# Loading decay weights as columns, doing the first decays in halves and moving an A product ahead of a broadcast, at the start of a fused RWKV-5 and MLP kernel

## The chip, the cores and the metric

One core of a Trainium2 chip (trn2). The metric is the device time of one execution in microseconds (us). Most executions agree within 0.3%, and the differences here are about 1% or less, so every experiment was timed beside the kernel before, in five rounds for most and three for e12.

Engines in the profile's lines: PE is TensorE, PEld its weight loads, DVE is VectorE, ACT is ScalarE, POOL is GpSimd, SP the sync engine, and a "q" behind a name is an engine's sequencer or queue. L12 is line 12 of that kernel's own file, so line numbers differ by a few between kernels.

## The reference, cut to what matters

```python
# r, k, v: (4 batches, 8 heads, 768 steps, 48); w, u: (8, 48)
for t in range(S):
    cur = np.einsum('bhd,bhe->bhde', u[None] * kt, vt)
    y[:, :, t] = np.einsum('bhd,bhde->bhe', rt, state + cur)
    state = w[None, :, :, None] * state + np.einsum('bhd,bhe->bhde', kt, vt)
# x: y as (3072, 384)
h = x @ w_in                       # w_in (384, 2048)
out = (h * (1.0 / (1.0 + np.exp(-h)))) @ w_out
```

The kernel works in chunks of 128 steps, 24 units (6 chunks by 4 batches). For each unit it decays r and k by powers of w, forms A = k r per head, masks it, and multiplies it with v; the term with u is the row sum of r (k u), times v. The MLP products fill TensorE between units.

## The kernel before

Only the start is touched. The tiles, the loads and the spins (products of zeros, there to get TensorE up to full pace):

```python
    wrow = cst.tile([NP, 2, 64], FP)
    urow = cst.tile([NP, 2, 64], FP)
    junk = cst.tile([128, 512], F16)
    nc.vector.memset(junk, 0.0)
    for t in (wrow, urow):
        nc.vector.memset(t[:, :, D:64], 1.0)
    ...
    load_row(wrow, w)
    load(0, mid=lambda: load_row(urow, u))      # r, k, u, v of unit 0 on the sync queue
    for i in range(1, B):
        load(i)
    ...
    spin(5)
    wT = to_cols(wrow, None)                    # transpose on TensorE
    spin(4)
    ...
    nc.vector.tensor_copy(out=pi[:, 0:NP, 1:2], in_=wT.unsqueeze(2))
    ...                                         # seven doublings: the powers of w and 1/w, "pif"
```

A spin is called cold here when the next one starts 0.43 us after it, and warm at 0.22 us. The granted-clock column of the profile reads 1.00 over these cold microseconds too, so in the first microseconds cold and warm are read from the spacing alone.

The two phases of a unit that matter, and the order in which unit 0 and 1 run:

```python
    def p1(i, mid=None, spins=0):               # r, k transposed, then decayed
        ...
        nc.vector.tensor_tensor(out=L["rT"], in0=tr[0:PR], in1=lamR, op=ALU.mult)
        if mid:
            mid()
        nc.vector.tensor_tensor(out=L["kT"], in0=tk[0:PR], in1=lamK, op=ALU.mult)
    # p2(i): A on TensorE into ae, ao; VectorE evicts both (copies them out) through the mask (am)
    # nat_ku, nat_rk: k*u and r*(k*u) on GpSimd; bonus_sum: row sums (rku) on VectorE
    ...
    p1(0, mid=to_cols_u)                        # u as a column, then "the rows of u": u repeated
                                                # on 128 partitions by TensorE; ScalarE copy: u_bc
    nat_v(0)
    ...                                         # lamCT on ScalarE
    nc.gpsimd.tensor_copy(out=gate, in_=rin[1][:, 0, 0:1])   # makes GpSimd wait for unit 1's r
    win_part(0, 512)                            # GpSimd issues a quarter of w_in
    nat_ku(0)
    nat_rk(0)
    p2(0)
    p1(1, spins=1)
    bonus_sum(0)
    nat_ku(1)
    nat_rk(1)
    nat_v(1)
    p3y(0)                                      # y of unit 0 on TensorE
    ...
    bonus_sum(1)
    bonus_vu(1)
    p2(1, spins=2)
    p3e(0)
    spin(4)
    p3y(1)
```

## Time and profile before

| | before |
|---|---|
| time, median of 4 runs | 201.77 us (201.52 to 202.05) |
| span of the profiled execution | 200.2 us |
| PE busy | 192.0 us, 96% |
| unit 0's r and k decays begin | 6.60 us |
| u's rows ready (u_bc) | 7.46 us |
| GpSimd's first ku begins | 8.75 us |
| unit 1's A eviction begins | 13.39 us |
| first MLP product begins | 17.13 us |

Times inside a span count from its first instruction. From 17 us on TensorE is the bound, and the rows from the decays down are the steps that lead there. Their profile lines stand in the prediction.

### The profile page before, as it was taken

The numbers are of one execution on the slowest core, as the hardware profiler recorded it, in microseconds if no ns is written. First come the engines' busy times: TensorE is split into PE (matmuls) and PEld (weight loads), VectorE is DVE, ScalarE is ACT, GpSimd is POOL, SyncE is SP. The second block draws the span as 40 slices with busy tenths as digits, with TensorE's granted clock in tenths as the row PEclk, the third lists the DMA queues.
The fourth block names the chain that finished last, engine by engine and source line by source line (L and its number), as shares of the span: only waits on it lengthen the run. The fifth ranks groups of instructions, "written<-read, shape, count | busy, mean of one in ns | idle before, by whom it ended". The sixth has DMA issues, their size and how long they took to land.

```text
span 200.2 us, 5013 instructions
## 1 busy us (share of the span) xinstructions
PE 192.0 (96%) x1973; PEld 129.8 (65%) x1973; DVE 115.1 (58%) x233; ACT 97.9 (49%) x225; POOL 115.2 (58%) x145
## 2 busy tenths in 40 slices
PE   7789999898999999999999999999999999999993
PEld 2546878786776976765666765666764666644563
DVE  6787658894757647773746864646863635510121
ACT  2655487798133652049662039662039661069300
POOL 3489969989865783768593767481748370100000
DMA  4999998999889954498521748201120001210022
GB/s 86 201 185 165 181 213 178 178 186 194 170 172 226 245 120 97 103 221 175 114 48 40 163 114 161 43 0 43 39 84 0 0 3 41 78 43 0 0 79 79
DMA packets 82207, 22.34 MB, mean 112 GB/s; under 512 B 75400, under 2 KB 82184, under 8 KB 82184
## 3 DMA queue, kind: packets, MB, share of 16 engines
q1 hardware_dynamic: 78504, 18.88, 43.7%
q0 software_dynamic: 3680, 3.15, 10.3%
q8 instruction: 15, 0.25, 0.5%
q14 instruction: 8, 0.07, 0.1%
HBM read 20.45 MB, written 4.72 MB: 126 GB/s over the span
## 4 chain that ended last, share of the span: by engine, by line
PE 84%; DVE 6%; POOL 4%; issue 3%; ACT 1%; DVEq 0%; POOLq 0%
PE ops L366 30%; PE hps L354 28%; PE ae L267 10%; PE xs L242 4%; PE y L293 3%; PE yT L342 2%; DVE am L276 2%; PE y L290 2%; POOL ku L180 1%; PE ops L380 1%; PE sps L309 1%; PE spin L125 1%; DVE pif L156 1%; POOL rku_f L186 1%; DVE y L300 1%
## 5 line engine op out<-in xcount | busy, mean ns | idle before, releaser
L357 ACT ACTIVATE gT<-hps 128x256 f16<-128x256 f32 (+1 forms) x128 | 59.5, 495 | 25.1 <-PE hps L354 23.3
L354 PE MATMUL hps<-xT,win 128*128 128x256 f16 (+1 forms) x384 | 69.9, 326 | 0.2
L366 PE MATMUL ops<-wout,gT 128*128 128x384 f16 x368 | 65.8, 326 | 0.0
L354 PEld LDWEIGHTS <-win 128*128 128x128 f16 x384 | 35.2, 98 | 22.1 <-issue 0.9
L366 PEld LDWEIGHTS <-gT 128*128 128x128 f16 x368 | 34.2, 98 | 20.9
L343 ACT COPY xT<-yT 128x384 f16<-128x384 f16 x24 | 11.5, 478 | 56.4 <-PE yT L342 56.4
L276 DVE TENSOR_TENSOR am<-ae,maskM 128x512 f16<-128x512 f32 x24 | 16.6, 691 | 32.5 <-PE ao L269 32.5
L203 POOL TENSOR_TENSOR vu<-vin,rku 128x384 f32<-128x384 f32 x23 | 19.1, 829 | 21.8 <-DVE rku L197 21.7
L370 DVE COPY osb<-ops 128x384 f32<-128x384 f32 x23 | 12.8, 556 | 32.5 <-PE ops L366 32.3
L267 PE MATMUL ae<-rk 48*128 48x128 f32 x192 | 27.7, 285 | 1.0 <-DVE rk L230 1.0
L267 PEld LDWEIGHTS ae<-rk 48*128 48x128 f32 x192 | 23.1, 187 | 8.3 <-issue 5.8
L269 PE MATMUL ao<-rk 48*128 48x128 f32 x192 | 27.7, 285 | 0.0
L253 DVE TENSOR_TENSOR rk<-xs,pif 112x512 f32<-112x512 f32 x40 | 25.6, 680 | 1.7 <-PE xs L242 1.7
L180 POOL TENSOR_TENSOR ku<-kin,u_bc 128x384 f32<-128x384 f32 x24 | 24.1, 1005 | 2.0 <-DMA kin<-in_k_dram 2.0
L186 POOL TENSOR_TENSOR rku_f<-rin,ku 128x384 f32<-128x384 f32 x24 | 24.1, 1005 | 1.9
L191 POOL TENSOR_TENSOR kc<-kin,lamC 128x384 f16<-128x384 f32 x24 | 24.0, 1002 | 0.0
L269 PEld LDWEIGHTS ao<-rk 48*128 48x128 f32 x192 | 23.1, 187 | 0.0
L323 POOL CAST stb<-st 112x384 f16<-112x384 f32 x12 | 6.0, 502 | 22.8 <-DVE st L318 22.8
L300 DVE TENSOR_TENSOR y<-y,vu 128x384 f16<-128x384 f32 x24 | 13.3, 554 | 8.7 <-PE y L293 6.5
L276 DVE TENSOR_TENSOR am<-ao,maskM 128x512 f16<-128x512 f32 x24 | 16.3, 680 | 0.0
L197 DVE TENSOR_REDUCE rku<-rku_f 128x8 f32<-128x384 f32 x24 | 13.2, 549 | 2.4 <-POOL rku_f L186 2.0
L325 POOL TENSOR_TENSOR sdec<-st,pif 112x384 f32<-112x384 f32 x16 | 13.3, 835 | 1.8 <-ACT gT L357 1.1
(74 smaller groups left out, 188.4 us busy)
## 6 DMA issues: line engine op xcount, KB each, us to landing
rin<-in_r_dram SPq DMA_DIRECT2D x24, 192.0 KB, 4.0
kin<-in_k_dram SPq DMA_DIRECT2D x24, 192.0 KB, 3.8
vin<-in_v_dram SPq DMA_DIRECT2D x24, 192.0 KB, 3.8
out_dram<-osb SPq DMA_DIRECT2D x23, 192.0 KB, 2.0
win<-in_moe_w_in_dram POOLq DMA_DIRECT2D x4, 384.0 KB, 6.0
wout<-in_moe_w_out_dram POOLq DMA_DIRECT2D x2, 768.0 KB, 10.4
out_dram<-osh SPq DMA_DIRECT2D x1, 128.0 KB, 1.7
out_dram<-osh SPq DMA_DIRECT2D x1, 64.0 KB, 1.5
```

What stands on the lines that cost most here:

```text
L180: nc.gpsimd.tensor_tensor(out=L["ku"], in0=kin[i % NIN][:, :, 0:D], in1=u_bc, op=ALU.mult)
L186: nc.gpsimd.tensor_tensor(out=L["rku_f"], in0=rin[i % NIN][:, :, 0:D], in1=L["ku"], op=ALU.mult)
L191: nc.gpsimd.tensor_tensor(out=kc[i % NKC][:, :, 0:D], in0=kin[n][:, :, 0:D], in1=lamC, op=ALU.mult)
L203: nc.gpsimd.tensor_tensor(out=L["vu"], in0=vin[i % NIN], in1=L["rku"].unsqueeze(2).broadcast_to([128, H, D]), op=ALU.mult)
L253: nc.vector.tensor_tensor(out=rk[:, :, :, 64 * g:64 * g + 64], in0=xs[g][0:PR], in1=lam(g), op=ALU.mult)
L267: nc.tensor.matmul(ae[:, p, :], L["kT"][0:D, p, :], L["rT"][0:D, p, :], start=True, stop=True)
L269: nc.tensor.matmul(ao[:, p, :], L["kT"][64:PR, p, :], L["rT"][64:PR, p, :], start=True, stop=True)
L276: nc.vector.tensor_tensor(out=am, in0=a, in1=maskM.unsqueeze(1).broadcast_to([128, NP, C]), op=ALU.mult)
L300: nc.vector.tensor_tensor(out=L["y16"], in0=L["y"], in1=L["vu"], op=ALU.add)
L354: nc.tensor.matmul(hps, win[:, q, ft * 128:(ft + 1) * 128], xts[sc][:, q, b0:b1, :].rearrange("p b t -> p (b t)"), start=(q == 0), stop=(q ...
L357: nc.scalar.activation(out=gts[sc][:, ft, b0 * C:b1 * C], in_=hps, func=AF.Silu)
L366: nc.tensor.matmul(ops, gts[sc][:, ft, b * C:(b + 1) * C], wout[:, ft, :], start=(ft == 0), stop=(ft == NFT - 1))
```

## The change

The intent: w arrives already as columns, so that no transpose and no wait for spins stands ahead of its powers; the first A product can start when half of the head pairs are decayed; and A goes ahead of the rows of u on TensorE so that it isn't held up by them.

```diff
-    wrow = cst.tile([NP, 2, 64], FP)
+    wcol = cst.tile([PR, NP], FP)
 ...
-    for t in (wrow, urow):
-        nc.vector.memset(t[:, :, D:64], 1.0)
+    nc.vector.memset(urow[:, :, D:64], 1.0)
+    nc.vector.memset(wcol[32:64, :], 1.0)
 ...
-    load_row(wrow, w)
+    for j, e in ((0, nc.sync), (1, nc.scalar)):
+        e.dma_start(out=wcol[64 * j:64 * j + D, :],
+                    in_=bass.AP(tensor=w.tensor, offset=D * j, ap=[[1, D], [PW, NP]]))
 ...
-    spin(5)
-    wT = to_cols(wrow, None)
-    spin(4)
+    spin(10)
 ...                                             # wT = wcol; in p1:
-        nc.vector.tensor_tensor(out=L["rT"], in0=tr[0:PR], in1=lamR, op=ALU.mult)
-        if mid:
-            mid()
-        nc.vector.tensor_tensor(out=L["kT"], in0=tk[0:PR], in1=lamK, op=ALU.mult)
+        step = NP // 2 if i == 0 else NP
+        for q in range(0, NP, step):
+            q = slice(q, q + step)
+            for x, t, lam_ in (("rT", tr, lamR), ("kT", tk, lamK)):
+                nc.vector.tensor_tensor(out=L[x][:, q], in0=t[0:PR, q], in1=lam_[:, q],
+                                        op=ALU.mult)
 ...
-    p1(0, mid=to_cols_u)
+    p1(0)
+    ucol = to_cols(urow, nc.scalar.copy)
+    p2(0)
+    to_rows(u_bc, lambda p: ucol[:, p:p + 1].broadcast_to([PR, 128]))
 ...
-    p2(0)
```

## The prediction

> **What bounds the kernel now.** I read the page first, then the merged chain of work that ended last, then the timeline of each engine over the first 17 us, because the diff touches nothing that runs later. The page's first part says what the rest of the run is:
>
> ```profile
> PE 192.0 (96%) x1973; PEld 129.8 (65%) x1973; DVE 115.1 (58%) x233; ACT 97.9 (49%) x225; POOL 115.2 (58%) x145
> ```
>
> TensorE is busy 96% of 200.2 us, and a table by stretches gives it 21.9 of 22.9 us between 17.1 and 40 and all of the time between 60 and 150. Its program order is fixed. So what the start loses or wins before about 17 us, where the first product of the MLP begins, should reach the end nearly one for one. The question is only when that point comes. The merged chain, start and duration in its first two columns, shows the path to it:
>
> ```profile
> 3.57 0.20 PE cols L129
> 3.79 0.17 DVE pif L152
> ...
> 6.60 0.70 DVE rk L226
> ...
> 8.76 1.01 POOL ku L180
> 9.84 1.00 POOL rku_f L186
> 10.84 0.96 POOL ku L180
> 11.89 1.01 POOL rku_f L186
> 12.92 0.55 DVE rku L197
> 13.47 1.21 DVE am L276 x2
> 14.72 0.35 PE y L293 x7
> ```
>
> The reader is to see two parts. To 7.3 us it is w: its transpose, the powers of w (pif), the decay of r and k (rk). From 8.76 to 12.9 it is GpSimd: two units' k times u and r times that. VectorE does unit 1's row sums (rku) ahead of its A eviction (am) in program order, so am waits for GpSimd, and so does y of unit 1. What GpSimd's first ku waited for is in its own timeline and in ScalarE's:
>
> ```profile
> 6.98 0.48 ACT L149 COPY u_bc<-rows 128x384 f32<-128x384 f32 x1 [0.69 <-PE rows L147]
> ```
>
> ```profile
> 7.67 0.19 POOL L430 COPY gate<-rin 128x1 f32<-128x1 f32 x1 [4.94 <-DMA rin<-in_r_dram]
> 7.79 0.93 POOL L413 DMA_DIRECT2D win<-in_moe_w_in_dram  x1
> 8.75 1.01 POOL L180 TENSOR_TENSOR ku<-kin,u_bc 128x384 f32<-128x384 f32 x1
> ```
>
> The rows of u were ready at 7.46, but GpSimd first waits for unit 1's r (7.67) and then issues a part of w_in for 0.93 us. So u had 1.3 us to spare. The chain names ScalarE's casts as the step before ku; that I read as an artefact, since the issue of a transfer is not counted as busy. VectorE's idle time confirms that unit 1 waited for GpSimd and not the reverse:
>
> ```profile
> 9.14 0.69 DVE L276 TENSOR_TENSOR am<-ae,maskM 128x512 f16<-128x512 f32 x1 [1.25 <-PE ao L269]
> ...
> 12.92 0.55 DVE L197 TENSOR_REDUCE rku<-rku_f 128x8 f32<-128x384 f32 x1 [0.83 <-POOL rku_f L186]
> ```
>
> VectorE sat idle 0.83 us for GpSimd. Unit 0's A eviction at 9.14 could come 0.8 us earlier and nothing would follow sooner.
>
> **What the Trainium skill says.** (1) DMA: Bandwidth & Descriptors, Rules for kernel authors: a strided last dimension becomes one descriptor per element. The w columns are such a load: 48 partitions by 4 single floats, 192 descriptors on each of two queues, against 8 pieces of 192 bytes before. No run of before has a load of this kind. (2) The same page, Where the ~2 µs actually goes: most of a small transfer's time is the confirmation of the last write, hardly its size. The trace agrees: w's packets moved at 2.33 to 2.45 us in the transfer view, but its transpose began at 3.50 though the weight-load engine had been idle 0.84 us; issued at 0.81, w took about 2.65 us, while unit 0's r, 128 times the bytes, took 2.7. (3) VectorE: DVE Perf Modes, the section on the TRN2 errata: each instruction pays a fixed cost beside its elements. The trace agrees: in the chain of powers 112x512 takes 0.70 us and 112x256 0.44, so 0.18 of fixed cost when dependent; independent 112x512 decays start 0.60 us apart. (4) TensorE: Matmul & The Clock Gate, Part 1: a cold array runs at half rate for about 3.4 us of work. The trace agrees at the start: the first spins' weight loads are 0.43 us apart (1.66, 2.09, 2.52), and the later ones closer.
>
> **The change part by part.**
>
> *w as columns.* Removed: the transpose on TensorE (3.50 to 3.77) and the wait of TensorE's five cold spins ahead of it. Added: a second queue and a wait. The built program's order shows what the diff does not: the column load on the sync queue waits for VectorE's memset of rows 32 to 64 of the same tile (rows 32 to 48 overlap). That is the third memset; the second started at 1.19 before, so the load is issued at about 1.30 in place of 0.81. With 2.65 us to landing it lands at 3.95. If the 0.82 us of the first issue was partly start-up (later issues took 0.42 to 0.66), take off up to 0.4; for 12 single-element descriptors per engine at the page's mean of 17.8 ns per packet (43.7% of 16 x 200.2 us over 78504 packets; an estimate) and the other queue's as many, add 0.2 to 0.4. I take 3.9, and the start of the powers at 3.95 against 3.79: **+0.15 us**. The ScalarE queue's half, issued near 0.8, should be there by 3.6. All r, k, u, v loads stand behind the waiting one and move 0.1 to 0.5 us later; r lands near 4.7 and k near 5.5, still ahead of the decay.
>
> *Decay in halves.* The powers take 2.68 us as before (3.79 to 6.47), so the decay begins at 6.6 + 0.15 = 6.75. Four instructions of half the size at about 0.35 us each: the first half of r and k is done at 7.45, the second at 8.15 (one pair of full size before: 1.2 us and ends at 7.9). The A product's first half runs 7.5 to 8.1 beside the second decays; its second half, half of the 1.15 us that eight pairs took before (7.95 to 9.10) plus a restart, runs 8.2 to 8.9. A's eviction starts near 8.95, against 9.14: **-0.2 us**, off the path.
>
> *A ahead of the rows of u.* This is the part that costs. The rows of u stood in TensorE's gap at 6.34, before the decay was done. Now they follow the second half of A: transposes from 8.75, 0.64 us until ScalarE starts (6.34 to 6.98 before), 0.48 for the copy: u is ready at about **9.9 instead of 7.46**. GpSimd is free at 8.75 plus what unit 1's r is late, say 9.0. So ku starts at 9.9 in place of 8.75, **+1.15 us**, and u has become its releaser.
>
> *Ten spins in one run.* Nine and a transpose become ten without a gap. Spins 6 to 8 stay cold, two run warm: end near 4.9, as the r transposes need r anyway: 0.
>
> *What follows.* From ku of unit 0 to the end of the second rku_f was 8.75 to 12.89 = 4.14 us, all GpSimd: now about 14.0; unit 1's sums 14.05, its A eviction 14.6 against 13.47, and y of unit 1 and all TensorE work behind it about 1.1 us later. ScalarE's casts and lamCT slide too (lamCT from 8.95 to 11.4, which holds the lamC transposes and unit 1's A product to about 13.3), still less than GpSimd's path. GpSimd itself gets back 0.58 us, its wait for unit 2's k at 15.07, but TensorE is then already late. Sum: +1.15 on the path, minus perhaps 0.1 absorbed later. 201.92 + 1.0 = **202.9 us**.
>
> **The rivals.** *It wins as intended* (the w part lands early and the A product releases everything): if both halves landed by 3.1, just after VectorE's memsets end at 2.96, the powers start 0.7 us sooner, the rows of u are ready at 9.2, and ku starts 0.4 late instead of 1.1. For a real gain the path from rku to am would have to be VectorE's own; the 0.83 us idle speaks against it. Time: 201.3 to 202.2. *It is absorbed*: GpSimd's waits for unit 2's k (0.58) and unit 4's k (1.43 us at 26.7) take up its delay and TensorE's fillers hide the rest. For it: DMA is at 98% or more through most of the first 17 us. Against it: y of unit 1 stands in front of the fillers in TensorE's fixed order, and TensorE idles under 1 us between 17 and 40. Time: about 202.0. *The columns are slow*: 4-byte descriptors from the two queues land 0.5 to 1 us later than I think and hold unit 0's r as well; every step above moves by that. Time: 203.5 to 204.
>
> **Range and chances.** The order of the built program makes u late in every case; the size hangs on the landing of w, between 3.2 and 4.6, that is -0.7 to +0.7 on 202.9. With a small chance that the delay is absorbed, the 8-in-10 range is 202.0 to 203.8. 2% is 4 us, far from any case here: within 2% 0.97, faster 0.01, slower 0.02. That it is above the time before I hold at 85%.
>
> **What would show it.** Right: the sync queue's w load starting at about 1.3; powers starting near 3.95; four decays of about 0.35; u's copy on ScalarE ending near 9.9 and GpSimd's first ku following it at once; VectorE idle before unit 1's rku well over 0.83 us; the first MLP product near 18.2 instead of 17.13. Wrong: powers starting before 3.4; ku of unit 0 at 8.8 or earlier; or all of that as predicted and the first MLP product, or the span, unmoved.

## The result, and the profile after

203.23 us (median of 4 runs, 202.92 to 203.40) against 201.77: the ratio is 1.0070, with a 95% interval of 1.0051 to 1.0090. Ratios here and below are the mean time of one kernel's runs over that of the other's of the same rounds, so not quite the ratio of the medians quoted. Executions over 1.5% slower than the fastest of the same kernel are left out of the means. Clear of noise it is 0.7% slower, 1.4 us. The granted clock of the profiled run is 0.999, so the two spans, 201.5 and 200.2 us, compare.

GpSimd's timeline of the changed kernel (start, duration, instruction, in brackets the idle time ahead of it and what ended it):

```profile
7.63 0.19 POOL L430 COPY gate<-rin 128x1 f32<-128x1 f32 x1 [4.90 <-DMA rin<-in_r_dram]
7.75 0.93 POOL L410 DMA_DIRECT2D win<-in_moe_w_in_dram  x1
10.15 1.00 POOL L179 TENSOR_TENSOR ku<-kin,u_bc 128x384 f32<-128x384 f32 x1 [1.46 <-ACT u_bc L147]
```

The gate and the issue stand where they were; ku comes at 10.15 in place of 8.75, after 1.46 us of idleness that u's copy ends. ScalarE's line for that copy, whose end is 9.58 + 0.48 = 10.06:

```profile
9.58 0.48 ACT L147 COPY u_bc<-rows 128x384 f32<-128x384 f32 x1 [2.12 <-PE rows L145]
```

VectorE's timeline of the changed kernel, in the order of the steps:

```profile
3.34 0.17 DVE L151 COPY pif<-wcol 112x4 f32<-112x4 f32 x1 [0.21 <-DMA wcol<-in_w_dram]
...
6.65 0.42 DVE L230 TENSOR_TENSOR rk<-tr,pif 112x256 f32<-112x256 f32 x1 [0.65 <-PE tr L222]
...
9.04 0.69 DVE L277 TENSOR_TENSOR am<-ae,maskM 128x512 f16<-128x512 f32 x1 [0.80 <-PE ao L270]
...
14.31 0.55 DVE L196 TENSOR_REDUCE rku<-rku_f 128x8 f32<-128x384 f32 x1 [1.49 <-POOL rku_f L185]
14.78 0.68 DVE L277 TENSOR_TENSOR am<-ae,maskM 128x512 f16<-128x512 f32 x1
```

Unit 0's A is evicted at 9.04 instead of 9.14, so the change did what it was meant to do there, by 0.1 us. Unit 1's sums wait 1.49 us for GpSimd, up from 0.83, and unit 1's A is evicted at 14.78 instead of 13.39. The two things that I had not expected are in the first two lines: the powers start at 3.34, earlier than before (3.79), but the decay then waits 0.65 us for the r transposes. TensorE's timeline says why:

```profile
1.26 4.45 PE L127 MATMUL spin<-junk 128*128 128x512 f16 x10 [1.26 <-DVE junk L80]
5.50 1.06 PE L222 MATMUL tr<-ident,rin 128*112 128x128 f32 x4
6.35 0.77 PE L222 MATMUL tk<-ident,kin 128*112 128x128 f32 x4
...
18.53 0.49 PE L355 MATMUL hps<-xT,win 128*128 128x256 f16 x3
```

All ten spins ran cold and the r transposes took 1.06 us. In the profile of the kernel before, the transposes began at 4.82 and four of them took 0.60 us:

```profile
4.82 0.60 PE L223 MATMUL tr<-ident,rin 128*112 128x128 f32 x4
...
17.13 0.49 PE L354 MATMUL hps<-xT,win 128*128 128x256 f16 x3
```

The first MLP product, 17.13 before, is at 18.53: 1.40 us later, which is the loss in the time.

### The profile page after: what moved, and what is told of

Same layout as the page of the kernel before. It is cut to its first block, busy times and chain, and to the rows that moved or that the text cites. A ratio compares the mean times of both kernels' runs of the same rounds, so it can differ in the third digit from the quotient of the medians.

```text
span 201.5 us, 5014 instructions
## 1 busy us (share of the span) xinstructions
PE 193.8 (96%) x1973; PEld 131.1 (65%) x1973; DVE 115.4 (57%) x235; ACT 97.7 (48%) x225; POOL 115.2 (57%) x145
## 3 DMA queue, kind: packets, MB, share of 16 engines
q0 software_dynamic: 3680, 3.15, 10.4%
## 4 chain that ended last, share of the span: by engine, by line
PE 83%; issue 6%; POOL 5%; DVE 4%; ACT 1%; POOLq 0%; DVEq 0%
PE ops L367 30%; PE hps L355 28%; PE ae L268 10%; PE xs L243 4%; PE y L294 3%; PE yT L343 2%; DVE am L277 2%; PE y L291 2%; POOL ku L179 1%; PE ops L381 1%; PE sps L310 1%; POOL rku_f L185 1%; DVE y L301 1%; PE ao L270 1%; DVE rku L196 1%
```

## The experiments

All are correct against the reference. "ku" is the start in the profile of unit 0's first GpSimd product with u, or of rku_f where ku was moved to VectorE.

| run | what it is | ku, us | time, us | ratio to before (95%) |
|---|---|---|---|---|
| the change | | 10.15 | 203.23 | 1.0070 (1.0051 to 1.0090) |
| e1 | change, u ahead of A | 8.60 | 201.72 | 0.9992 (0.9980 to 1.0004) |
| e2 | w part alone | 8.48 | 201.79 | 0.9996 (0.9983 to 1.0009) |
| e3 | before, GpSimd delayed 1 us | 9.79 | 202.74 | 1.0053 (1.0028 to 1.0077) |
| e4 | order part alone | 10.25 | 203.93, two groups | 1.0101 (1.0080 to 1.0122) |
| e7 | e4, eight spins later on | 10.25 | 203.34 | 1.0079 (1.0066 to 1.0092) |
| e10 | change, eight spins | 9.44 | 202.47 | 1.0030 (1.0016 to 1.0044) |
| e6 | before, ku on VectorE | (8.68) | 201.60 | 0.9987 (0.9975 to 0.9999) |
| e8 | e2, ku on VectorE | (8.83) | 201.15 | 0.9971 (0.9959 to 0.9983) |
| e5 | e1, ku on VectorE | (9.59) | 201.11 | 0.9970 (0.9950 to 0.9991) |
| e9 | e5, eight spins | (8.77) | 201.06 | 0.9958 (0.9946 to 0.9971) |
| e11 | e8, eight spins | (8.55) | 201.06 | 0.9957 (0.9945 to 0.9970) |
| e12 | before, three spins then six | 8.93 | 201.96 | 1.0007 (0.9990 to 1.0024) |

My theory after the result: the loss is u reaching GpSimd late, and nothing else. The rivals: the cold spins and late transposes (the w part) cost it, or the halves do.

**e1, the changed kernel with u's rows ahead of A again.**

```diff
-    p2(0)
     to_rows(u_bc, lambda p: ucol[:, p:p + 1].broadcast_to([PR, 128]))
+    p2(0)
```

> The changed kernel with one thing undone: the rows of u stand ahead of unit 0's A product again. Theory (the loss is u reaching GpSimd late, 10.15 in place of 8.75 us): the u column is transposed near 7.05 as in the changed kernel, its rows near 7.6, ScalarE's copy ends near 8.7, so GpSimd's first ku starts at 8.7 to 8.9 and the time is 201.6 to 202.1 us, all of the loss gone. Rival (the loss is the cold spins, the late r transposes or the halves): ku may come early, but the time stays at 202.8 us or more.

201.72 us, and ku at 8.60: the whole loss is gone with the early w, the ten spins and the halves still in place. (u itself was ready at 8.03, earlier than I had expected, because in this profile the transposes ran warm.) GpSimd is again bound by its own gate and issue:

```profile
7.64 0.94 POOL L410 DMA_DIRECT2D win<-in_moe_w_in_dram  x1
8.60 1.01 POOL L179 TENSOR_TENSOR ku<-kin,u_bc 128x384 f32<-128x384 f32 x1
```

**e2, the w part alone.** The edit is the change's diff without the loop over q and without the move of p2(0).

> The kernel before with the w part alone: columns on two queues and ten spins in one run, decays whole, rows of u ahead of A. Theory: the powers start near 3.35 but the r transposes, behind ten cold spins, hold the decay to about 6.6; ku starts at 8.7 to 8.9; time 201.6 to 202.2 us. Rival (the w part and its cold spins are what cost): 202.8 us or more.

201.79 us: the columns and the ten spins cost nothing that is clear of noise. They also win nothing, although unit 0's A is evicted 0.33 us sooner (8.81 against 9.14).

**e4, the order part alone.** The edit is the last two hunks of the change's diff, on the kernel before.

> The kernel before with the order part alone: w as rows, whole decays, the rows of u behind unit 0's A product. Theory: A ends at 9.1 as before, u's rows run 9.0 to 9.6, the copy ends near 10.1, ku starts near 10.15, time 203.0 to 203.4 us: the whole loss. Rival (the w part or the halves cost): 201.6 to 202.2 us.

The order alone makes the whole loss and more: ku waits for u in this kernel too.

```profile
10.25 1.00 POOL L180 TENSOR_TENSOR ku<-kin,u_bc 128x384 f32<-128x384 f32 x1 [1.61 <-ACT u_bc L149]
```

Its six executions fell into two groups, though: 203.34, 203.47, 203.33, and 204.51, 204.39, 204.43. Only the first group is what I had expected. All six count by the 1.5% rule, so the ratio in the table mixes the two; the lower group alone, 203.38 on average, is 0.75% above the kernel before. The record has a mean granted clock for each execution: 1.000 for the three lower ones, 0.991 to 0.992 for the three upper ones. So in the upper group the clock fell somewhere.

**e3, GpSimd delayed by 1 us in the kernel before.**

```diff
+    dly = cst.tile([128, H, D], FP)
+    nc.gpsimd.tensor_tensor(out=dly, in0=kin[0][:, :, 0:D], in1=rin[0][:, :, 0:D],
+                            op=ALU.mult)
     nat_ku(0)
```

> The kernel before with one extra product of ku's shape (1.0 us) on GpSimd just ahead of unit 0's ku, its result unused. Theory (a delay on GpSimd's first chain reaches the end one for one): ku starts at 9.8, the first MLP product at about 18.2 in place of 17.13, time 202.7 to 203.0 us. Rival (GpSimd's later waits and TensorE's fillers absorb it): 202.2 us or less.

202.74 us: a delay of 1.04 us on GpSimd alone (9.79 against 8.75) brought 0.8 us by the medians and 1.1 by the means. So most or all of it reaches the end, which the rival had denied. The mean is raised by one execution of 204.29 us, with a granted clock of 0.992. It is the profiled one, and its TensorE timeline shows what happened:

```profile
16.76 1.06 PE L223 MATMUL tr<-ident,rin 128*112 128x128 f32 x4
17.61 1.06 PE L223 MATMUL tk<-ident,kin 128*112 128x128 f32 x4
```

These are unit 2's transposes, four in each line, which take 0.60 us in the kernel before. The table by stretches of the same profile (stretch, its length, busy time and count of PE, PEld, DVE, ACT and POOL, then the granted clock, the DMA share and GB/s) has the clock at half for more than three microseconds:

```profile
14.00:15.00 1.00, 0.00 (x0) 0.00 (x0) 1.00 (x2) 0.81 (x3) 0.98 (x2) 1.00 1.09 220
15.00:16.00 1.00, 0.44 (x7) 0.34 (x8) 1.00 (x3) 0.00 (x0) 1.00 (x2) 0.86 0.63 93
16.00:17.00 1.00, 1.00 (x12) 0.79 (x10) 0.72 (x2) 0.00 (x0) 0.92 (x2) 0.50 0.78 114
...
19.00:20.00 1.00, 1.00 (x7) 0.32 (x5) 0.86 (x2) 0.89 (x2) 1.00 (x2) 0.93 1.15 214
```

TensorE had just stood idle for 1.35 us ahead of y of unit 1 (0.31 in the kernel before), because GpSimd was late, and for 0.40 us more inside it (as in the kernel before). The first products of this y, here and in the kernel before:

```profile
15.16 0.20 PE L293 MATMUL y<-v,am 128*128 128x48 f16 x1 [1.35 <-DVE am L276]
```

```profile
14.12 0.20 PE L293 MATMUL y<-v,am 128*128 128x48 f16 x1 [0.31 <-DVE am L276]
```

Up to here the delay was passed on whole: 1.04 us. The half clock then put the first MLP product at 19.56, where 18.2 was expected.

**e7, the order-only kernel with that gap filled.**

```diff
     p3e(0)
-    spin(4)
+    spin(8)
     p3y(1)
```

> The order-only kernel, whose executions fell into two groups (203.3 to 203.5 and 204.4 to 204.5 us), with eight spins in place of four in TensorE's gap ahead of y of unit 1, which the late u made longer. Theory (in the second group the array's clock dropped during that gap and the matmuls behind it ran at half rate): the second group is gone, all executions at 203.2 to 203.6 us. Rival (the two groups have another cause): executions near 204.4 remain.

203.31 to 203.46 us in all five, with granted clocks of 0.999 to 1.000: the upper group is gone. That the upper group was a fall of the clock is shown by its granted clocks; that the fall came in this gap is supported by e7 and by the profile of e3, but no execution of e4's upper group was profiled. The gap does not always do it: the changed kernel has the same two gaps (1.01 and 0.40 us) and none of its four executions fell, nor did any of e10's five (0.99 and 0.40 us).

**e10, the changed kernel with two spins fewer.**

```diff
-    spin(10)
+    spin(8)
```

> The changed kernel with eight spins in place of ten. In its profile the ten spins ran cold to the end, 0.43 us each, and the r transposes could start only at 5.50 us, 0.65 us after VectorE had the powers ready. Theory (the spins took back what the early w had given): two spins fewer start the r transposes at 4.65 to 4.75, the decay at 6.1 to 6.4, u is ready near 9.6 in place of 10.06, and the time is 202.6 to 202.9 us. Rival (unit 0's r or k lands too late for that, or the array stays cold longer for want of spins): decay at 6.6 or later, 203.1 us or more.

202.47 us, with the decay at 6.11 instead of 6.65, u ready at 9.35 instead of 10.06 and ku at 9.44:

```profile
9.44 1.00 POOL L179 TENSOR_TENSOR ku<-kin,u_bc 128x384 f32<-128x384 f32 x1 [0.68 <-ACT u_bc L147]
```

The two last spins and the cold transposes took back 0.7 us of what the early w had given, and since u stands behind A in this kernel, that reached the end: about half of the loss (ratio 1.0030 instead of 1.0070). So in the changed kernel the spins are part of the loss too, by way of u. Its executions lie within 0.06 us; those of the changed kernel spread over 0.48.

**e12, when w really lands.** I had read the start of w's transpose, 3.50, as w's landing.

```diff
-    spin(5)
+    spin(3)
     wT = to_cols(wrow, None)
-    spin(4)
+    spin(6)
```

> The kernel before with three spins ahead of w's transpose and six behind it, in place of five and four. I had read the transpose's start at 3.50 us as the landing of w. But the powers start at 3.79 in every profile of a kernel with w as rows and anywhere from 3.30 to 3.42 with columns, so the fixed time may be that of five cold spins. If the spins held it: the transpose starts at 2.6 to 3.2 us and the powers at 3.0 to 3.5. If w's landing held it: transpose at 3.5 and powers at 3.8 as before. The time stays at 201.5 to 202.1 us in both cases, since GpSimd's ku at about 8.7 sets the path.

```profile
2.89 0.22 PE L129 MATMUL cols<-ident,wrow 4*112 4x4 f32 x1 [0.17 <-DMA wrow<-in_w_dram]
```

With two spins fewer ahead of it the transpose started at 2.89, and the profile names w's transfer as what it then waited for. The semaphore records in the packed traces, which no view prints for this transfer, settle it: the last increment for w comes at 2.76 here and at 2.75 in the kernel before, 1.94 us after the issue at 0.81. So in the kernel before it was the five cold spins that held the transpose until 3.50. The powers started at 3.15. The time did not move (ratio 1.0007), although the r transposes, cold here (1.06 us from 5.58), made u the releaser of ku, at 8.93 and not at 8.7.

**e5, e6, e8: is there a gain behind GpSimd?** Unit 0's ku goes to VectorE, which idles there.

```diff
-        nc.gpsimd.tensor_tensor(out=L["ku"], in0=kin[i % NIN][:, :, 0:D], in1=u_bc,
-                                op=ALU.mult)
+        e = nc.vector if i == 0 else nc.gpsimd
+        e.tensor_tensor(out=L["ku"], in0=kin[i % NIN][:, :, 0:D], in1=u_bc, op=ALU.mult)
```

In e6 this is the only edit to the kernel before; e8 is e2 with it; e5 is e1 with it, where the call also moves ahead of p2(0).

> The kernel before with unit 0's ku moved from GpSimd to VectorE, nothing else. Theory: GpSimd's part ends 1.0 us earlier (near 11.9), but unit 1's A product, which ends at 12.7 in the kernel before, now sets the eviction: 12.75 in place of 13.39, time 201.1 to 201.5 us; less is won than with the w columns and halves. Rival as in the run beside it: 201.7 us or more.

> The w part alone (columns, ten spins, decays whole, u ahead of A) with unit 0's ku on VectorE. It lies between the two runs beside it: against the one without columns it shows what the early w gives once GpSimd does not hide it, against the one with halves what the halves give. Theory: A's eviction near 8.8, 0.3 us ahead of the kernel before and 0.2 behind the halves; time 200.9 to 201.4 us. Rival (neither gives anything): equal to the run without columns within 0.1 us.

> The changed kernel with the rows of u ahead of A (as the first experiment) and, besides, unit 0's ku moved from GpSimd to VectorE, into its idle time before A's eviction. Theory (GpSimd's chain alone hid what the early w and the halves give): GpSimd starts with rku_f at 8.6, ends unit 1's rku_f near 11.7 in place of 12.7, unit 1's A eviction starts near 12.3 in place of 13.2, and the time is 200.7 to 201.2 us, below both kernels. Rival (something else, such as unit 2's k landing near 15 us, binds there): 201.6 us or more.

201.60, 201.15 and 201.11 us. e6 wins a little less than I had expected: GpSimd finishes 1.2 us earlier, but unit 1's eviction moves only to 12.87, as its A product now ends last:

```profile
12.87 0.69 DVE L276 TENSOR_TENSOR am<-ae,maskM 128x512 f16<-128x512 f32 x1 [0.33 <-PE ao L269]
```

With the columns (e8) another 0.45 us comes by the medians, 0.34 by the means, and no execution of the one overlaps with the other's: the early w is worth something once GpSimd doesn't hide it. e5 is the miss: its rku_f began at 9.59, not 8.6, because in its profile the transposes ran cold to 7.4 and u with them, and its six executions spread from 200.58 to 201.91.

**e9 and e11: eight spins, with and without the halves.** The edit is e10's, on e5 and on e8.

> Columns, halves, rows of u ahead of A, unit 0's ku on VectorE, and eight spins. With ten spins the executions spread from 200.6 to 201.9 us, and in the profile the r and k transposes ran cold to 7.4. Theory (that spread is when the array's clock goes up, and fewer spins leave the transposes time even cold): spread under 0.7 us, median 200.5 to 201.0 us. Rival (the spread has another cause): as wide as before, median 201.1 us.

> The same without the halves: columns, whole decays, rows of u ahead of A, unit 0's ku on VectorE, eight spins. Beside the run with halves it shows what the halves are worth where nothing hides them. Theory: the first two half decays end 0.5 us before two whole ones, but A ends only 0.2 us earlier, so the run with halves is 0.1 to 0.3 us faster; this one 200.8 to 201.2 us. Rival: no difference within 0.1 us, since rku_f from GpSimd and not A sets unit 1's eviction.

201.06 us both, spreads of 0.37 and 0.34 us. With halves, eight spins narrow the spread from 1.33 us (e5), as expected, though the median stays just above the expected 200.5 to 201.0. Without halves there was nothing to narrow: e8's five executions, with ten spins, lie within 0.28 us. So ten spins alone do not make a wide spread. The halves are worth nothing, against my expectation. One reason is that, with u's rows ahead of A, TensorE is busy with them until the whole decays are done. TensorE's lines for the first part of A, with halves (e9) and without (e11):

```profile
6.89 0.60 PE L145 MATMUL rows<-ident,cols_sb 112*128 112x112 f32 x4 [0.25 <-ACT cols_sb L134]
7.42 0.37 PE L268 MATMUL ae<-rk 48*128 48x128 f32 x1
```

```profile
7.46 0.37 PE L268 MATMUL ae<-rk 48*128 48x128 f32 x1 [0.26 <-DVE rk L231]
```

The rival's reason is not excluded: in e9's profile VectorE waits 0.30 us for GpSimd's second rku_f before unit 1's eviction at 12.34, and unit 1's A ends at that time too (the spin behind it starts at 12.24, 0.10 us ahead of the eviction, as in e11, where A alone sets it). So the two are tied there.

e9 and e11 have the lowest medians found, with ratios 0.42 and 0.43% below the kernel before; their intervals overlap with those of e5 and e8. e11 is the simpler: w as columns, eight spins, ku of unit 0 on VectorE, and the order of before.

## Why the prediction was right, and where it was not

The time, 202.9 predicted and 203.23 measured, and its cause held. Step by step:

| step | predicted | measured in the changed kernel |
|---|---|---|
| sync queue's w load issued (waits for the memset) | 1.30 | 1.36 |
| powers of w start | 3.95 | 3.34 |
| spins end, r transposes start | near 4.9 | 5.50 |
| decay starts | 6.75 | 6.65 |
| last half decay ends | 8.15 | 8.25 |
| unit 0's A evicted | 8.95 | 9.04 |
| u ready | 9.9 | 10.06 |
| second rku_f ends | 14.0 | 14.28 |
| unit 1's A evicted | 14.6 (on the chain's scale) | 14.87 on that scale, 14.78 in the timeline |
| first MLP product | 18.2 | 18.53 |

**Right.** The part that costs is A ahead of the rows of u: e4 makes the loss alone and e1 takes it away alone. The chain behind ku took 4.13 us (10.15 to 14.28) where I had taken 4.14. The loss passes on nearly one for one: ku 1.40 us later, first MLP product 1.40 later, time 1.4. The 0.1 us that I had let later waits absorb was not absorbed, and ku came 0.25 us later than the 9.9 that I had forecast. Together they make up 0.35 of the 0.4 us by which the loss exceeded the 1.0 forecast.

**Wrong: the landing of w.** "w took about 2.65 us" rested on the start of its transpose. It took 1.94 us; the rest of the wait ahead of the transpose was for the spins (e12). With it falls the remark that the trace agrees with the skill on where a small transfer's time goes: of the 1.94 us, 1.56 passed before w's first packet moved (2.37) and 0.30 after its last had (2.46). With columns, the sync queue's part landed 1.9 us after its issue by the transfer list, single floats and all, so the powers came 0.45 us earlier than before and not 0.15 later. The fear in the third rival, that 4-byte pieces are slow, fell with it.

**Wrong: the spins, taken as 0.** I let two of the ten run warm. In this profile none did, and they and the cold transposes held the decay to 6.65, where the powers allowed 6.1 as in e10. The four half decays then took 1.60 us and not 1.40, as the first one of k waited for the cold k transposes (7.16). The two mistakes, -0.6 and +0.55, cancelled at the decay, so the steps behind it came out within 0.35 us. That is luck, and a reader should not take the agreement as proof of the first steps: it took e10 and e12 to find them.

**Of the rivals,** the winning one had named its own obstacle rightly: the early w was there, and GpSimd hid it (e2). Absorption is refuted by e3: a delay of 1.04 us cost 0.8 by the medians (the 1.1 by the means includes the fall of the clock).

## What to carry to other kernels

Before moving an instruction ahead of another in one engine's fixed order, ask who waits for the one that is pushed back: here the rows of u had 1.3 us to spare and were pushed back by 2.6, and the engine behind them was the one that set the path. An engine that reaches a product earlier wins nothing while another engine's chain ends later; relieve that chain first (ku on VectorE), and only then is the early start worth measuring. And a transfer's landing cannot be read from the start of its first user while that user has something else to wait for.

## What the Trainium skill lacked or had wrong

- TensorE: Matmul & The Clock Gate, Part 1, has the clock go up around 4 us into sustained matmuls, give or take 0.5 us, and says that the number of cold matmuls varies from run to run. It varies more widely here. Spins start at 1.26 in all kernels, and with the same instructions so far the pace doubled between the spins at 4.09 and 4.36 in e7's profile, about 3 us in, while e3's last four were all cold (1.89 us against 1.27). In the changed kernel the r transposes were still cold until 6.35, 5.1 us in (1.06 us for four); those of e8, behind the same ten spins, were warm at 5.23 (0.60 us). So a fixed number of warm-up spins on the path costs a varying time.
- The same page, Why this matters for your kernels, wants no TensorE-idle gaps over about 3 us, since a window of idle time lowers the clock again. Shorter gaps can do it: in e3's profile 1.35 and 0.40 us of idle time, with one short product between them, were followed by a granted clock of 0.50. (The page's section on psum-queue depth-cycling has frequent short idles do it too, but gives no length.) e4 has gaps of 1.01 and 0.40 us in the profile, and half of its executions took 1.1 us more (204.4 against 203.4) at a granted clock of 0.991 to 0.992; with four more spins in the first gap (e7) none did. What else it takes is open, since the changed kernel with the same gaps did not fall in four executions.
- DMA: Bandwidth & Descriptors has one descriptor per element for a strided last dimension and advises against it. The count agrees (208 packets on the ScalarE queue for 192 floats), but it gives no time for a load of this kind: here it landed 1.8 to 1.9 us after issue, no later than the same floats in rows (1.94 us).
- The same page, Where the ~2 µs actually goes, puts most of a small transfer's fixed time behind its last byte. The table stands under the GpSimd path; for w in rows on the sync queue 1.56 of 1.94 us came before the first packet and 0.30 behind the last.
- No page that I read says that the weight load of a 4-row transpose behind full-array spins does not run ahead of them as others do: w's began at 3.50 with its matmul, though w had landed at 2.75, while the r transposes' weight load began at 4.61, 0.21 us ahead of their matmul. The reason is open.
